# Output gate before reciprocal: VectorE multiplies numerator and gate into x's tile, GpSimd scales by the reciprocal in place

## Chip, cores and metric

One core of a Trainium2 chip runs the whole kernel. The metric is the device time of one execution in microseconds, as the median of three runs. TensorE's granted clock is full (1.0) over the whole profiled execution.

## What is computed

An attention-like recurrence (mLSTM) over 4 batches, 8 heads, 768 positions and head dimension 40, then a soft mixture of experts, then a feed-forward block. The change lies in the first part. Cut to what matters:

```python
for t in range(S):
    C = f_stab * C + i_stab * outer(v_t, k_t)
    n = f_stab * n + i_stab * k_t
    h_tilde = C @ q_t
    denom = max(abs(n . q_t), 1.0)
    o = 1 / (1 + exp(-o_gate_t))
    y[t] = o * h_tilde / denom           # the product that the change regroups
x = y as (3072 tokens, 320)
logits = x @ phi ; d = softmax over tokens ; slot_input = d.T @ x ; ...
```

The kernel computes the recurrence chunk by chunk. For every token it gets a numerator row (320 values and, per head, one value for the denominator), the reciprocal of the denominator (8 values), and the sigmoid of the output gate (320 values); x is the product of the three.

## The kernel before

The 3072 tokens are 24 units of 128 tokens: 6 chunks of the sequence times 4 batches, unit u = 4 * chunk + batch. The loop over iterations i = 0 to 23 is software-pipelined by hand. Iteration i works on units i-2 to i+2 at once, and the order in which the steps are issued is a string of step names: `FIRST` for iterations 0 to 5, `ORDER[i % 4]` for 6 to 21, `LAST` for 22 and 23. Each engine executes its own instructions strictly in the order in which the strings issue them, and waits on semaphores where a tile is not ready or not free. I call an iteration by its kind, i mod 4, and four iterations a period.

The steps that matter, with engine and line in the kernel before:

- `numa`, `numb` (VectorE, L327 and L329): the numerators of unit i-1, from TensorE's sums `pr` and `po` in PSUM, into `num`, of which there is one tile. `po` and `pr` are one PSUM tile each, so TensorE's first product of the next unit into `po` waits for `numb`.
- `den0`, `den2` (VectorE, L337 and L341): denominator and reciprocal `rd` of unit i-1; two `rd` tiles in turn.
- `sg` (VectorE, L345): sigmoid of the output gate times `rd`, in place in the tile `kvo` (or `kvl`) of the unit.
- `x` (GpSimd, L360): `num` times that product, into the unit's x tile. There are five x tiles, unit u has tile u mod 5 (names `x` and `xx` in the rows).
- `xT` (TensorE, L365): transposes x of unit i-2.
- `sl` (TensorE, L439), in iterations of kind 2: the slot sums of four units that are complete, which read their x tiles. In iteration i they read the x tiles of units i-6 to i-3, and the x written in the same iteration is that of unit i-1. Unit i-1 and unit i-6 have the same x tile.
- `acc` (VectorE, L447, the first time L445): adds the slot sums, in iterations of kind 2.
- `scA`, `scB` (TensorE, L280): scores of unit i+1; `wA`, `wB` (VectorE, L284): scores times decay, into `lb`. The score tiles in PSUM are single, so the next `scA` waits for both.
- `o0` to `o3` (TensorE, L298 and L301): outputs of unit i from `lb` and the state. `u0` to `u3` (L308): state updates.
- `cd` (GpSimd, L316): decayed state; `C` (VectorE, L356): the new state. `kw` (GpSimd, L269): weights on the keys of unit i+1, read by `u0` to `u3` of the next iteration.
- `D0` to `D4`: decoding of a weight tile, over two iterations. `D0` (L477, L478), `D3` (L486) and `D2` (L484) are VectorE's, `D1b` and `D1` ScalarE's, `D4` (L488) GpSimd's.
- L200 and L202 (VectorE, in `gate`): two small gate steps at the start of iterations 8, 12 and 16.

All loads are issued by SyncE in program order, ahead of their use. After iteration 23 come the expert part (a short stretch bound by TensorE and by what each step hands to the next) and the feed-forward part over 24 units.

The x step of the kernel before reads:

```python
x = x_t[u % NX]
(V if u == NU - 1 else EE("x")).tensor_tensor(out=x[:, 0:DM]..., in0=U[u]["num"][:, :, 0:D], in1=U[u]["sg"], op=ALU.mult)
```

Of the kernel before, what the change touches and what calls it, by code (L numbers as in the profile page):

```python
# [14 lines left out]
ALU = mybir.AluOpType  # L15
# [3 lines left out]
NB, NH, S, D = 4, 8, 768, 40  # L19
T = TOK = 128  # L20
NC = S // T
NU = NB * NC
NR = NH // 2
DV = D + 1
DM = NH * D
# [5 lines left out]


ORDER = (
# [4 lines left out]
)  # L38
LAST = (
 "numa xT tm1 scA numb scB den0 xTc tm2 nt ntc sig0 R o0 den2 o1 exp sg sig1 kw o3 wA wB o2 sl qm x sig2",  # L40
# [2 lines left out]
FIRST = (  # L43
# [6 lines left out]
)  # L50
# [6 lines left out]
FIN = "o:-1 u:2 d:2 t:2 h:3 m:3 q:0 k0:0 T0:1 T1:1 k1:0 x0:1 g:1 x1:1 y1:0 y0:1 k2:0 k3:0 s:0 a4:0 a5:0 e:3 a6:0 a7:0 v:1 b4:0 b5:0 b6:0 b7:0"  # L57
DT = range(2, 24)
HALF = (slice(0, 64), slice(64, 128))
ENG = {"x": "G", "cd": "G", "kw": "G", "sg": "V", "D4": "G", "C": "V", "xTc": "A"}  # L60


@with_exitstack
def tile_kernel(
# [13 lines left out]
    nc = tc.nc  # L78
    EE = lambda n: {"V": nc.vector, "G": nc.gpsimd, "A": nc.scalar}[ENG[n]]
    V, A, G, PE, SP = nc.vector, nc.scalar, nc.gpsimd, nc.tensor, nc.sync  # L80
# [19 lines left out]
    acc = cpool.tile([128, DM + 1], F32, tag="acc", name="acc")  # L100
# [24 lines left out]
    def fixed(name, shape, n=1, dtype=F32):  # L125
        t = [p1.tile(shape, dtype, tag=f"{name}{i}", name=f"{name}{i}") for i in range(n)]
        return t if n > 1 else t[0]

    NX = 5
    x_t = fixed("x", [128, 384], 2)  # L130
# [42 lines left out]
    U = [dict() for _ in range(NU)]  # L173
# [157 lines left out]
    def st_den(u, k):  # L331
# [8 lines left out]
        else:  # L340
            V.reciprocal(out=rd, in_=rd)  # L341

    def st_sg(u):
        sg = U[u]["kvo"][:, 2 * DM + NH:].rearrange("p (h d) -> p h d", h=NH)
        EE("sg").tensor_tensor(out=sg, in0=sg, in1=U[u]["rd"].unsqueeze(2).to_broadcast([128, NH, D]), op=ALU.mult)  # L345
        U[u]["sg"] = sg

    def st_state(u):
# [7 lines left out]
            V.tensor_tensor(out=C_t[b][0:n], in0=U[u]["cd"][0:n], in1=dps[0:n], op=ALU.add)  # L356

    def st_x(u):
        x = x_t[u % NX]
        (V if u == NU - 1 else EE("x")).tensor_tensor(out=x[:, 0:DM].rearrange("p (h d) -> p h d", h=NH), in0=U[u]["num"][:, :, 0:D], in1=U[u]["sg"], op=ALU.mult)  # L360

    def pe_xT(u):
        ps = ps_o.tile([128, 512], F32, tag="misc", name=f"xTp{u}")
# [257 lines left out]
    def ops(i):  # L621
# [13 lines left out]
        if prv:  # L635
            T["numa"] = lambda: st_num(i - 1, (0,))
            T["numb"] = lambda: st_num(i - 1, (1,))
            T["C"] = lambda: st_state(i - 1)
            for k in range(3):
                T[f"den{k}"] = lambda k=k: st_den(i - 1, k)  # L640
            T["sg"] = lambda: st_sg(i - 1)
            T["x"] = lambda: st_x(i - 1)
# [100 lines left out]
    def bank(tag, name):  # L743
        return ps_o.tile([128, 512], F32, tag=tag, name=name)
# [8 lines left out]
    U[L]["sg"] = kvo_t[L % 4][:, 2 * DM + NH:].rearrange("p (h d) -> p h d", h=NH)  # L753
    st_den(L, 0)
    st_x(L)
    st_den(L, 2)
    xl = x_t[L % NX][:, 0:DM].rearrange("p (h d) -> p h d", h=NH)
# [6 lines left out]
    xT = U[L]["xT"] = xT_t[L % 4]  # L764
# [9 lines left out]
    st, lt = gst_t[g % 2], lg[:, 0:128]  # L774
# [17 lines left out]
    sl = [bank(t, f"sl_last{k}") for k, t in enumerate(("dps", "po"))]  # L792
# [275 lines left out]
    for t in FIN_START.split():  # L1068
        op, i = t.split(":")
# [3 lines left out]
    for i in range(NU + 1):  # L1073
        for t in FIN.split():
            op, d = t.split(":")
# [78 lines left out]
```

## Time and profile before

| | us |
|---|---|
| median of 3 runs | 287.72 (286.51 to 288.02) |
| the profiled execution | 284.2 |
| its span, first to last instruction | 282.4 |

| engine | busy us | share of the span |
|---|---|---|
| TensorE, matmuls | 267.7 | 95% |
| VectorE | 243.1 | 86% |
| ScalarE | 216.9 | 77% |
| GpSimd | 149.6 | 53% |

The shares are averages over stages. Iterations 6 to 21, which the change touches, lie at about 39 to 126 us of the span; 16 of the 24 units are gone through there, in four periods of about 21.5 us. The feed-forward part fills the span from about 166 us on and issues its own instructions, which the change leaves as they are. What the change does to the time is therefore read from the four periods: which engine is waited for there, and where.

### The profile page before, as it was taken

To read this page: it belongs to the slowest core of one execution; us is meant where nothing else is said; L and a number is where in the kernel's file an instruction comes from. 1 tells how busy PE (TensorE), PEld (TensorE's weight loads), DVE (VectorE), ACT (ScalarE), POOL (GpSimd) and SP (SyncE) were. 2 spreads that over 40 slices of the span, in tenths; PEclk is the share of its full clock that TensorE was granted. 3 is DMA by queue.
4 is the path that set the end of the run, shared out by engine and by line. 5 is a ranking of instruction groups with operands and counts; after the bars stand their busy time and mean duration, and the time that the engine had idled before them with its cause. 6 is when DMAs were issued, how large, how long until landed. Compare 5 with 4: busy or idle time off the path is not lost.

```text
span 282.4 us, 8484 instructions
## 1 busy us (share of the span) xinstructions
PE 267.7 (95%) x3293; PEld 216.9 (77%) x3293; DVE 243.1 (86%) x514; ACT 216.9 (77%) x513; POOL 149.6 (53%) x179
## 2 busy tenths in 40 slices
PE   8899989999999999999899998999999999999995
PEld 5676767777777776867533367998999999999994
DVE  7999787998998997996579699999999999899950
ACT  6798957998789786797436758996877878778763
POOL 5754433654555555348106400556868767676760
PEclk9999999999999999999999999999999999999999
DMA  5898997999999998999999100246445364443531
GB/s 156 276 290 296 311 318 277 317 300 269 296 313 285 300 282 263 295 260 381 364 362 360 51 0 2 60 89 129 106 94 111 84 99 100 91 105 94 99 86 46
DMA packets 48808, 56.63 MB, mean 201 GB/s; under 512 B 26816, under 2 KB 38720, under 8 KB 48768
## 3 DMA queue, kind: packets, MB, share of 16 engines
q1 hardware_dynamic: 48768, 56.09, 67.6%
q8 instruction: 26, 0.43, 0.6%
q14 instruction: 14, 0.11, 0.1%
HBM read 46.38 MB, written 3.93 MB: 178 GB/s over the span
## 4 chain that ended last, share of the span: by engine, by line
PE 78%; DVE 6%; ACT 5%; issue 4%; DMA 4%; POOL 3%; POOLq 0%; ACTq 0%; SPq 0%; DVEq 0%
PE o L1046 9%; PE o L1043 9%; PE o L1044 9%; PE sc L280 8%; PE po L298 7%; PE R L244 4%; PE pr L301 4%; PE uT L1008 4%; PE h L962 3%; PE ph L836 3%; PE xTp L365 3%; PE so_ps L893 3%; DMA w2s<-w 3%; PE R L247 2%; PE dps L308 2%
## 5 line engine op out<-in xcount | busy, mean ns | idle before, releaser
L1043 PE MATMUL o<-wh,uh 128*128 128x320 f32 x192 | 60.3, 320 | 0.3 <-POOL uh L1029 0.3
L1044 PE MATMUL o<-wl,uh 128*128 128x320 f32 x192 | 58.2, 309 | 0.0
L1046 PE MATMUL o<-wh,ul 128*128 128x320 f32 x192 | 47.9, 310 | 0.1
L1014 POOL COPY up<-u 128x1024 uint16<-128x1024 uint16 x22 | 23.3, 1058 | 33.4 <-issue 16.1
L1024 POOL COPY uf<-tp 128x1024 uint16<-128x1024 uint16 x22 | 32.1, 1458 | 10.2 <-DMA tp<-up 10.1
L1043 PEld LDWEIGHTS o<-wh,uh 128*128 128x128 f32 x192 | 36.1, 188 | 1.5 <-POOL uh L1029 0.6
L1044 PEld LDWEIGHTS o<-wl,uh 128*128 128x128 f32 x192 | 36.1, 188 | 0.9
L1046 PEld LDWEIGHTS o<-wh,ul 128*128 128x128 f32 x192 | 33.0, 188 | 0.6 <-DVE ul L1035 0.6
L284 DVE TENSOR_TENSOR lb<-sc,lb 128x512 f32<-128x512 f32 x48 | 31.1, 674 | 1.9 <-PE sc L280 1.9
L967 DVE TENSOR_REDUCE st<-h 128x1 f32<-128x1024 f32 x24 | 29.2, 1220 | 0.3 <-PE h L962 0.2
L298 PE MATMUL po<-kvo,lb 128*64 128x41 f32 x544 | 27.2, 227 | 2.0 <-issue 2.0
L253 ACT ACTIVATE lb<-R 64x512 f32<-64x512 f32 (+1 forms) x48 | 25.5, 580 | 2.7 <-PE R L247 2.6
L1050 ACT ACTIVATE ob<-o,st 128x320 f32<-128x320 f32 x24 | 12.7, 529 | 18.9 <-ACT ga L974 8.4
L298 PEld LDWEIGHTS po<-kvo,lb 128*64 128x64 f32 x544 | 22.4, 137 | 5.1 <-issue 3.4
L280 PE MATMUL sc<-qk 64*128 64x128 f32 x288 | 23.1, 289 | 0.0
L280 PEld LDWEIGHTS sc<-qk 64*128 64x128 f32 x288 | 18.6, 187 | 4.2 <-issue 2.7
L1035 DVE TENSOR_TENSOR ul<-uf,uh 128x512 fp32r<-128x512 f32 x22 | 20.7, 941 | 1.2 <-POOL uh L1029 1.2
L981 DVE SCALAR_TENSOR_TENSOR u<-h,ga 128x1024 f32<-128x1024 f32 (+1 forms) x17 | 19.6, 1157 | 2.0 <-ACT ga L974 1.8
L1035 DVE TENSOR_TENSOR ul<-uT,uh 128x512 fp32r<-128x512 f32 x26 | 17.8, 684 | 2.8 <-ACT uh L1031 2.7
L261 ACT ACTIVATE kvo<-kvo 128x320 f32<-128x320 f32 x36 | 17.0, 472 | 3.8 <-DMA kvo<-kvo 1.9
L301 PE MATMUL pr<-C,qk 128*64 128x82 f32 x224 | 19.5, 249 | 0.0
L244 PE MATMUL R<-gr,gl 128*128 128x512 f32 x48 | 17.3, 442 | 1.1 <-ACT lb L253 1.1
(285 smaller groups left out, 708.9 us busy)
## 6 DMA issues: line engine op xcount, KB each, us to landing
w1s<-w1p SPq DMA_DIRECT2D x19, 512.0 KB
w2s<-w SPq DMA_DIRECT2D x7, 1280.0 KB
kvo<-kvo SPq DMA_DIRECT2D x15, 484.0 KB
out<-ob SPq DMA_DIRECT2D x24, 160.0 KB
qk<-qkp SPq DMA_DIRECT2D x18, 160.0 KB
qk<-qkp SPq DMA_DIRECT2D x36, 80.0 KB
kvl<-kvo SPq DMA_DIRECT2D x5, 484.0 KB
raw<-w SPq DMA_DIRECT2D x4, 512.0 KB
```

Source lines behind the costliest of these rows:

```text
L244: PE.matmul(U[u]["R"][:, a], gl_t[c % 2][:, b, :], gr_t[c % 2][:, a * NR:(a + 1) * NR, :], start=True, stop=False)
L253: A.activation(out=lb[p, :, :, t], in_=U[u]["R"][p, :, :, t], func=AF.Exp)
L280: PE.matmul(U[u]["sc", a][:, r, :], t[p, 0, r, :], t[p, 1, r, :], start=True, stop=True)
L284: V.tensor_tensor(out=lb[:, a * NR:(a + 1) * NR, :], in0=U[u]["sc", a], in1=lb[:, a * NR:(a + 1) * NR, :], op=ALU.mult)
L298: PE.matmul(U[u]["po"][t, 2 * r + a, 0:DV], U[u]["lb"][:, a * NR + r, t], va(u, 2 * r + a), start=not last or r + a == 0, stop=not last)
L301: PE.matmul(U[u]["po" if last else "pr"][t, 2 * r:2 * r + 2, 0:DV], qk_t[u % 4][:, 1, r, t], C_t[b][:, r, :].rearrange("p (a d) -> p a d", ...
L967: V.tensor_reduce(out=F[i]["st"][:, 0:1], in_=F[i]["h"], axis=AX.XY, op=ALU.max, negate=True)
L1024: G.tensor_copy(out=uf.rearrange("p k t -> p (k t)").bitcast(U16).rearrange("p (n two) -> p n two", two=2), in_=F[i]["tp"].rearrange("p tw ...
L1035: V.tensor_tensor(out=F[i]["ul"][:, c, :], in0=F[i]["uT", n], in1=F[i]["uh"][:, c, :].bitcast(F32), op=ALU.subtract)
L1043: PE.matmul(o, uh, wh[:, k, :], start=k == 0, stop=False)
L1044: PE.matmul(o, uh, wl[:, k, :], start=False, stop=False)
L1046: PE.matmul(o, ul, wh[:, k, :], start=False, stop=k == FC - 1)
```

## The change

In units 5 to 20 the three factors of x are grouped in another way. Before, VectorE multiplied gate and reciprocal (`sg`), and GpSimd multiplied the numerators by that. Now `sg` stands for VectorE's product of numerators and gate, written into the unit's x tile, and `x` for GpSimd's multiplication of that tile by the reciprocal, in place. The number of instructions on each engine stays as it was. The first five and the last three units keep the old grouping.

The order strings move with it. `sg` goes directly behind `numb` in kinds 0, 1 and 3; in kind 2 it stays behind `sl`. `x` goes to directly behind the reciprocal (or, in kind 2, behind `sg`), and `cd` goes ahead of `x`; `kw` and `D4` stand behind `x` on GpSimd where they had stood ahead of it.

```diff
@@ ORDER @@
- "R D1b D1 sig0 numa D2 scA C xT scB numb den0 den1 o0 u0 xTc left exp den2 wB o3 o2 gn sg wA cd o1 gnc sig1 x D0 u1 u2 u3 kw sig2 right",
- "D1b xT C numa numb R scA D1 den0 den1 xTc D3 den2 sig0 right left D2 scB kw sg wA o0 wB x u1 cd o3 lt o2 sig1 u3 o1 u2 D4 exp lraw ltc u0 tm0 sig2",
- "numa D1b xT tm1 scA numb D1 C scB den0 xTc tm2 D2 nt ntc sig0 den1 R o0 den2 o1 gn gnc sl sg sig1 u3 kw o3 wA wB cd o2 x exp acc u1 u2 u0 D0 sig2 right",
- "D1b xT numa R C numb scA D3 D1 scB o0 den0 sig0 cd den1 u3 D2 den2 wA D4 o3 u0 sig1 sg exp wB xTc u1 u2 o1 o2 lraw x sig2 kw right",
+ "R D1b D1 sig0 numa D2 scA C xT scB numb sg den0 den1 o0 u0 xTc left exp den2 cd wB o3 o2 gn x wA o1 gnc sig1 D0 u1 u2 u3 kw sig2 right",
+ "D1b xT C numa numb sg R scA D1 den0 den1 xTc D3 den2 cd sig0 right left D2 scB x kw wA o0 wB u1 o3 lt o2 sig1 u3 o1 u2 D4 exp lraw ltc u0 tm0 sig2",
+ "numa D1b xT tm1 scA numb D1 C scB cd den0 xTc tm2 D2 nt ntc sig0 den1 R o0 den2 o1 gn gnc sl sg x sig1 u3 kw o3 wA wB o2 exp acc u1 u2 u0 D0 sig2 right",
+ "D1b xT numa R C numb sg scA D3 D1 scB o0 den0 sig0 cd den1 u3 D2 den2 x wA D4 o3 u0 sig1 exp wB xTc u1 u2 o1 o2 lraw sig2 kw right",
...
@@ ENG: one entry more @@
+ "gate": "V"
...
+    def xh(u):
+        return x_t[u % NX][:, 0:DM].rearrange("p (h d) -> p h d", h=NH)
+
+    def rd_wide(u):
+        return U[u]["rd"].unsqueeze(2).to_broadcast([128, NH, D])
+
+    def early(u):
+        return len(FIRST) - 1 <= u < NU - 3
+
     def st_sg(u):
         sg = U[u]["kvo"][:, 2 * DM + NH:].rearrange("p (h d) -> p h d", h=NH)
-        EE("sg").tensor_tensor(out=sg, in0=sg, in1=U[u]["rd"].unsqueeze(2).to_broadcast([128, NH, D]), op=ALU.mult)
+        if early(u):
+            EE("gate").tensor_tensor(out=xh(u), in0=U[u]["num"][:, :, 0:D], in1=sg, op=ALU.mult)
+            return
+        EE("sg").tensor_tensor(out=sg, in0=sg, in1=rd_wide(u), op=ALU.mult)
         U[u]["sg"] = sg
...
     def st_x(u):
-        x = x_t[u % NX]
-        (V if u == NU - 1 else EE("x")).tensor_tensor(out=x[:, 0:DM].rearrange("p (h d) -> p h d", h=NH), in0=U[u]["num"][:, :, 0:D], in1=U[u]["sg"], op=ALU.mult)
+        if early(u):
+            EE("x").tensor_tensor(out=xh(u), in0=xh(u), in1=rd_wide(u), op=ALU.mult)
+        else:
+            (V if u == NU - 1 else EE("x")).tensor_tensor(out=xh(u), in0=U[u]["num"][:, :, 0:D], in1=U[u]["sg"], op=ALU.mult)
```

How this moves instructions, at two places. First VectorE, from the reciprocal of iteration 10 (kind 2) into iteration 11 (kind 3). The columns are line, operation, output and inputs, size, and the engines whose semaphores it waits for. Before:

```order
L341 RECIPROCAL rd_113<-rd_113 128x8 [waits DVE_49]
L345 TENSOR_TENSOR kvo_117<-kvo_117,rd_113 128x320 [waits DMAHW7_49,DVE_49]
L284 TENSOR_TENSOR lb_0_124<-sc_0_1113,lb_0_124 128x512 [waits PE_49]
L284 TENSOR_TENSOR lb_0_124<-sc_1_1114,lb_0_124 128x512 [waits PE_49]
L447 SCALAR_TENSOR_TENSOR acc<-acc,gst_102,sl_1157 128x321 [waits PE_49,Activation_49]
L477 TENSOR_SCALAR dsc_118<-raw_96 128x512 [waits DMAHW3_49,Pool_49]
L478 TENSOR_SCALAR wo<-raw_96 128x512
L327 TENSOR_TENSOR num_114<-pr_1143,nat_110 128x8x41 [waits PE_49,Pool_49]
L356 TENSOR_TENSOR C_122<-cd_119,dps 104x328 [waits PE_49]
L329 TENSOR_TENSOR num_114<-num_114,po_1142 128x8x41 [waits DVE_49]
L486 SCALAR_TENSOR_TENSOR dsc_118<-raw_96,dsc_118 128x512 [waits Activation_49]
L337 TENSOR_REDUCE rd_112<-num_114 128x8 [waits DVE_49]
```

The same stretch in the changed kernel (L355 is the product of numerators and gate, L461 is `acc`, L368 `C`, L500 and L498 are `D3` and `D2`):

```order
L341 RECIPROCAL rd_113<-rd_113 128x8 [waits DVE_49]
L355 TENSOR_TENSOR xx_100<-num_114,kvo_117 128x320 [waits DMAHW7_49,PE_49]
L284 TENSOR_TENSOR lb_0_124<-sc_0_1113,lb_0_124 128x512
L284 TENSOR_TENSOR lb_0_124<-sc_1_1114,lb_0_124 128x512
L461 SCALAR_TENSOR_TENSOR acc<-acc,gst_102,sl_1158 128x321 [waits PE_49,Activation_49]
L491 TENSOR_SCALAR dsc_118<-raw_96 128x512 [waits DMAHW3_49,Pool_49]
L492 TENSOR_SCALAR wo<-raw_96 128x512
L327 TENSOR_TENSOR num_114<-pr_1144,nat_110 128x8x41 [waits DVE_49,PE_49]
L368 TENSOR_TENSOR C_122<-cd_119,dps 104x328 [waits PE_49,Pool_49]
L329 TENSOR_TENSOR num_114<-num_114,po_1143 128x8x41 [waits DVE_49]
L355 TENSOR_TENSOR x_94<-num_114,kvo_116 128x320 [waits DMAHW5_49,DVE_49]
L500 SCALAR_TENSOR_TENSOR dsc_118<-raw_96,dsc_118 128x512 [waits Activation_49]
```

Before, L345 at the first place touches only `kvo` and `rd`, and behind `numb` of iteration 11 comes `D3`. Now L355 writes `xx_100` there and waits for PE, ahead of the two `lb` instructions and `acc`; a second L355 stands between `numb` and `D3`, and no instruction stands between `lb`'s two halves any more.

Second GpSimd, at the same place: from `cd` of iteration 10 to `kw` of iteration 11. Before:

```order
L316 TENSOR_TENSOR cd_119<-C_122,nat_110 104x328 [waits DVE_49]
L360 TENSOR_TENSOR xx_100<-num_114,kvo_117 128x320 [waits DVE_49,PE_49]
L316 TENSOR_TENSOR cd_119<-C_123,nat_110 104x328 [waits DVE_49,Pool_49]
L488 TENSOR_TENSOR wo<-wo,dsc_118 128x512 [waits DVE_49]
L360 TENSOR_TENSOR x_94<-num_114,kvo_116 128x320 [waits DVE_49,PE_49,Activation_49]
L269 TENSOR_TENSOR kvl_130<-kvl_130,nat_111 128x320 [waits DMAHW0_49]
```

In the changed kernel (L372 is the multiplication by the reciprocal, L502 is `D4`):

```order
L316 TENSOR_TENSOR cd_119<-C_122,nat_110 104x328 [waits DVE_49]
L372 TENSOR_TENSOR xx_100<-xx_100,rd_113 128x320 [waits DVE_49]
L269 TENSOR_TENSOR kvo_115<-kvo_115,nat_110 128x320 [waits DMAHW2_49]
L316 TENSOR_TENSOR cd_119<-C_123,nat_110 104x328 [waits DVE_49]
L372 TENSOR_TENSOR x_94<-x_94,rd_112 128x320 [waits DVE_49,PE_49]
L502 TENSOR_TENSOR wo<-wo,dsc_118 128x512
L269 TENSOR_TENSOR kvl_130<-kvl_130,nat_111 128x320 [waits DMAHW0_49,Activation_49]
```

Before, `D4` came ahead of x of iteration 11 and waited for VectorE on its own; now x comes first and `D4` directly ahead of `kw`. The `kw` of iteration 10 (on `kvo_115`) stood ahead of these rows and now stands behind the x of that iteration.

## Rows read from the trace of the kernel before

**Rows 1.** Busy time by engine in one period of four iterations, columns named.
```profile
core 0: us, PE busy (x) PEld busy (x) DVE busy (x) ACT busy (x) POOL busy (x), PEclk, DMA share, GB/s
...
79.30:100.80 21.50, 20.87 (x396) 16.30 (x395) 20.58 (x45) 18.18 (x49) 11.98 (x15) 1.00 0.96 293
```

**Rows 2.** Waits of VectorE, 36 to 127 us: total us, times, longest.
```profile
DVE acc L447 <- PE sl L439: 3.3, 3, 1.5
DVE acc L445 <- PE sl L439: 2.1, 1, 2.1
DVE num L327 <- POOL xx L360: 0.4, 1, 0.4
```

**Rows 3.** VectorE's instructions, 59 to 76 us: start, duration, line, tiles, wait before.
```profile
59.24 0.68 DVE L486 SCALAR_TENSOR_TENSOR dsc<-w1s,dsc 128x512 int32<-128x512 int32 x1
...
60.51 0.48 DVE L345 TENSOR_TENSOR kvl<-kvl,rd 128x320 f32<-128x320 f32 x1
60.91 1.28 DVE L284 TENSOR_TENSOR lb<-sc,lb 128x512 f32<-128x512 f32 x2
...
63.93 0.20 DVE L341 RECIPROCAL rd<-rd 128x8 f32<-128x8 f32 x1
...
64.85 1.27 DVE L284 TENSOR_TENSOR lb<-sc,lb 128x512 f32<-128x512 f32 x2
67.27 0.55 DVE L447 SCALAR_TENSOR_TENSOR acc<-acc,gst,sl 128x321 f32<-128x321 f32 x1 [1.15 <-PE sl L439]
...
69.27 0.48 DVE L329 TENSOR_TENSOR num<-num,po 128x328 f32<-128x328 f32 x1
69.67 1.09 DVE L486 SCALAR_TENSOR_TENSOR dsc<-raw,dsc 128x512 int32<-128x512 int32 x1
70.69 0.16 DVE L337 TENSOR_REDUCE rd<-num 128x8 f32<-128x16 f32 x1
...
72.04 1.11 DVE L345 TENSOR_TENSOR kvo<-kvo,rd 128x320 f32<-128x320 f32 x1
73.08 0.68 DVE L284 TENSOR_TENSOR lb<-sc,lb 128x512 f32<-128x512 f32 x1
73.68 0.59 DVE L200 TENSOR_TENSOR ga<-ga 32x128 f32<-32x128 f32 x1
74.20 0.70 DVE L202 TENSOR_TENSOR dec<-cst,ga 32x16 f32<-32x16 f32 x1
...
75.64 0.48 DVE L329 TENSOR_TENSOR num<-num,po 128x328 f32<-128x328 f32 x1
```

**Rows 4.** TensorE's instructions at the same place, columns alike.
```profile
66.61 0.43 PE L439 MATMUL sl<-xx,dn 128*32 128x321 f32 x1
...
68.18 0.55 PE L365 MATMUL xTp<-cst,xx 128*128 128x128 f32 x3
...
76.22 0.43 PE L298 MATMUL po<-kvl,lb 128*64 128x41 f32 x8 [0.58 <-PE sc L280]
...
88.04 0.44 PE L439 MATMUL sl<-x,dn 128*32 128x321 f32 x2
```

**Rows 5.** GpSimd's instructions at the same place, columns alike.
```profile
67.11 0.81 POOL L360 TENSOR_TENSOR xx<-num,kvo 128x320 f32<-128x320 f32 x1 [1.59 <-PE sl L439]
69.49 0.73 POOL L316 TENSOR_TENSOR cd<-C,nat 104x328 f32<-104x328 f32 x1 [1.57 <-DVE C L356]
71.53 1.27 POOL L488 TENSOR_TENSOR wo<-wo,dsc 128x512 f32<-128x512 f32 x1 [1.31 <-DVE wo L484]
73.32 0.80 POOL L360 TENSOR_TENSOR x<-num,kvo 128x320 f32<-128x320 f32 x1 [0.52 <-DVE kvo L345]
74.08 0.79 POOL L269 TENSOR_TENSOR kvl<-kvl,nat 128x320 f32<-128x320 f32 x1
```

**Rows 6.** TensorE in iterations 20 and 21.
```profile
119.12 0.43 PE L298 MATMUL po<-kvl,lb 128*64 128x41 f32 x8
...
121.46 0.55 PE L365 MATMUL xTp<-cst,xx 128*128 128x128 f32 x3 [0.62 <-POOL xx L360]
```

More of the change, by code (lines that the diff above doesn't have):

```diff
@@ L59 @@
 HALF = (slice(0, 64), slice(64, 128))
-ENG = {"x": "G", "cd": "G", "kw": "G", "sg": "V", "D4": "G", "C": "V", "xTc": "A"}
+ENG = {"x": "G", "cd": "G", "kw": "G", "sg": "V", "gate": "V", "D4": "G", "C": "V", "xTc": "A"}
 @with_exitstack
```

## Prediction

> **What bounds the kernel now.** I read the stage table first. In iterations 6 to 21 TensorE is busy 20.87 of 21.50 us in a period, VectorE 20.58, and the DMA engines 0.96 of the time [rows 1]; none has room for much. So the question is not what an engine has to do, but who waits for whom. VectorE's waits come next: it waits nearly only at one place, once in each of the four periods, in front of `acc` for TensorE's slot sums `sl`: 2.1 us in the first period and 3.3 us in the other three together [rows 2]. Third I laid the instructions of VectorE, TensorE and GpSimd side by side from iteration 10 to 14 and looked for the loop that sets the period.
>
> It is this. `sl` of iteration 10 ends at 66.61 + 0.43 = 67.04 [rows 4]. `acc` starts 0.23 later at 67.27, and from there VectorE works without a gap until `numb` of iteration 12 ends at 75.64 + 0.48 = 76.12 [rows 3]. TensorE has then been idle for 0.58, because the one `po` tile is not free before `numb` has read it, and goes on 0.10 later at 76.22; without another gap it ends `sl` of iteration 14 at 88.04 + 0.44 = 88.48 [rows 4]. 0.23 + 8.85 + 0.10 + 12.26 = 21.44 us, which is the period. Whatever is put on VectorE between `sl` and that `numb` lengthens it one to one. Ahead of `sl`, on the other hand, VectorE has time to spare: the reciprocal of iteration 10 is done at 63.93 + 0.20 = 64.13, and `sg` and both `lb` products stand between it and `acc` and are done while `sl` is still coming [rows 3].
>
> **What the change does to that loop.** The change adds no instruction and removes none; it moves work from one side of `sl` to the other.
>
> *Kind 2.* The new VectorE product writes the x tile that `sl` of the same iteration is still reading (unit i-1 and unit i-6 share it). Before, that wait was GpSimd's, whose x started at 67.11 after 1.59 us of waiting [rows 5]; now it is VectorE's, and behind the waiting instruction are queued both `lb` products and `acc`. VectorE would be there at 64.13 and stands until about 67.11. Then come the product (0.40 from start to start, as `sg` from 60.51 to 60.91) and two `lb` products (0.60 each, 73.08 to 73.68) [rows 3], and `acc` starts at 67.11 + 0.40 + 1.20 = 68.71 instead of 67.27: **+1.44 us**. The same instructions used to be hidden by the wait; that cover is gone.
>
> *Kind 3.* From `acc` to `numb` of iteration 11 nothing changes (2.00 us, to 69.27) [rows 3], so `numb` starts at 70.71. The product behind it has two inputs in SBUF, and `cd` starts on GpSimd 0.22 behind `numb` and takes 0.73 [rows 5]. Two such instructions do not run side by side: the `sg` of 72.04 met `D4` (71.53 + 1.27 = 72.80), took 1.11 instead of 0.48 and ended 0.35 after it [rows 3, 5]. So `cd` lasts to 71.66, the product to 72.01, and it costs 71.94 - 71.11 = +0.83. In exchange `D3`, which stood beside `cd` with 1.09, is back to 0.68: -0.41. And `sg` between the `lb` halves goes, with 73.08 - 72.04 = -1.04 [rows 3]. Sum -0.62, balance +0.82: the second `lb` half is done and L200 is reached at 74.50 instead of 73.68.
>
> *L200 and L202* open iterations 8, 12 and 16. They meet GpSimd too: L202, 16 columns wide, takes 0.70 beside `kw`, and ends 0.03 behind it (74.90 and 74.87) [rows 3, 5]. In the new order x starts on GpSimd about 0.17 after the reciprocal (about 73.4, as the first `lb` half begins), so at about 73.55; `D4` 0.76 behind it at 74.3, until 75.58. L200 arrives 0.2 too late for the gap and ends 0.15 behind `D4` (as behind x before), at 75.73; `kw` then runs from 75.54 to 76.33 and L202 ends at 76.36 instead of 74.90: +0.64 more, balance **+1.46**. `numb` ends at 77.58, TensorE's `o0` starts at 77.68, and the period is 21.44 + 1.46.
>
> The Trainium skill has a rule for these meetings ("SBUF — State Buffer", section "Who interferes with whom"): a VectorE instruction with two SBUF inputs and a GpSimd instruction that reads SBUF exclude each other for the whole instruction, and the one that issues first goes first. The rows on `sg` and `D4` agree. By that rule L200 waits for all of `D4`, as in my sum; if the two could overlap, the sum would be +2.7 instead of +4.6.
>
> *Kinds 0 and 1.* There the product behind `numb` replaces `sg` behind the reciprocal, and in kind 0 `cd` meets it. All this lies on the part of the loop where TensorE is without a gap and VectorE arrives at the next `sl` some 2.5 us early, so I cost it at nothing.
>
> *What else moves.* x of kind 2 comes later (product, then GpSimd, about 68.5); the transposition that reads it starts at 68.18 [rows 4] and waits some 0.4, but TensorE has to wait longer than that for `numb` of iteration 11 a little later, so nothing. `kw` in kind 2 comes after x instead of before it, at about 69.2, ahead of the state updates that read it. In the other kinds x is done earlier. The wait of `num` for GpSimd disappears, 0.4 us in all [rows 2]. The `kvo` tile is free earlier, so SyncE's loads are issued earlier or at the same time.
>
> **The sum.** Three whole loops (`sl` of 6 to 10, 10 to 14, 14 to 18; the others show the pattern of the one I laid out, the `acc` wait of each included): 3 x 1.46 = 4.4. The fourth ends in iteration 20, which has no L200 and L202: TensorE's `o0` at 119.12 comes 0.82 later; but its 0.62 wait for x at 121.46 [rows 6] goes, since x no longer comes behind `sg`: +0.2. Together **+4.6 us**. After that everything (the last units, the loads for the expert part, which wait for tiles that TensorE frees, and the feed-forward part) follows TensorE and shifts as a whole. On the profiled execution's 284.2 us this makes 288.8; that execution lies 3.5 below the median of the runs shown, and with the same shift the median goes from 287.72 to **292.3**.
>
> **Rivals.**
>
> *A, smaller.* L200 slips in front of `D4`, or `D4` is late itself. Then 3 x 0.82 + 0.2 = +2.7: 290.4. For it: the order is decided by 0.2 us. Against: `D4` then holds L202 instead.
>
> *B, larger.* `kw` goes ahead of L200 as well (+0.3), VectorE wakes as late after `sl` as `acc` does (67.27 instead of 67.11, +0.16), and the wait in iteration 21 is not regained: 3 x 1.92 + 0.82 = +6.6: 294.3.
>
> *C, no change.* The loads set the pace, and compute only waits elsewhere. For it: DMA busy share 0.96 [rows 1]. Against: TensorE goes on 0.10 behind VectorE's `numb`, not behind a load. Then 287.7.
>
> *D, faster.* The wait for `sl` never shows, because VectorE comes to the product after `sl`. Then only the gains stay: 0.62 in each of three loops and the 0.62 of iteration 21, 287.72 - 2.5 = 285.2. It decides at VectorE being 67.04 - 64.13 = 2.9 us later at that place than now; nothing moves it by so much, since VectorE's delay delays `sl` as well.
>
> **How the numbers follow.** Forecast 60%, A 15%, B 12%, C 8%, D 5%. The predicted time is the forecast's, 292.3. The range holds A and B and leaves out C and D, with 0.8 below A and 0.3 above B, since the runs themselves lie 1.5 apart: 289.6 to 294.6. This kernel's measurement can tell about 0.5% (1.4 us) from no change. Faster by more than that: D, 5%. Within it: C and the lowest of A, 10%. Slower: 85%.
>
> **What would show it.** Right: in the profile after, VectorE's line for the new product is the one that waits for `sl`, nearly 3 us each of four times, and `acc` no longer waits; from `sl` of 10 to `sl` of 14 are 22.9 us instead of 21.44; `o0` of iteration 12 starts 0.1 behind `numb` and after an idle time of over 1 us; L200 and L202 together take over 1.7 us; the product in kind 3 takes about 0.9, `D3` 0.68. Wrong: no wait at the product (D), or a period of 21.4 with the wait there (C), or TensorE stopped somewhere else, for instance at the state updates for `kw`, which I have cost at nothing.

## The result, and the profile after

The changed kernel takes 288.53 us (median of 20 runs, 286.67 to 293.27), the kernel before 285.74 beside it (median of 20 runs, 283.10 to 290.96). The ratio is 1.0106 [1.0076, 1.0137]: 3.0 us slower, 2.2 to 3.9 (the ratio's ends less 1, times 285.74). The sign and the place were as predicted; 288.53 lies below the range of 289.6 to 294.6. Medians here are over all runs, and ratios over those that lie within 1.5% of their kernel's fastest, so the two differ a little.

In the profile that is shown here, TensorE waited 1.7 us for late loads of `qk` in iteration 6 and then had a granted clock of 0.50 for 3.4 us. Up to these loads both kernels issue the same instructions, so I compare from the end of `sl` in iteration 6 on. I call the stretch from the end of one `sl` to the end of the next a loop; there are three, and the prediction's is the middle one. Busy time by engine in the three loops of the kernel before (the first column is the stretch, the first number behind it its length):

```profile
core 0: us, PE busy (x) PEld busy (x) DVE busy (x) ACT busy (x) POOL busy (x), PEclk, DMA share, GB/s
45.13:67.04 21.91, 21.17 (x398) 16.54 (x398) 20.61 (x44) 19.78 (x54) 11.94 (x14) 1.00 0.92 293
67.04:88.48 21.44, 20.86 (x399) 16.36 (x399) 20.51 (x44) 17.77 (x47) 11.91 (x14) 1.00 0.95 298
88.48:110.59 22.11, 21.08 (x398) 16.38 (x399) 20.32 (x44) 17.46 (x46) 11.97 (x14) 1.00 0.95 288
```

The same view of the changed kernel:

```profile
49.98:72.59 22.61, 20.65 (x399) 16.11 (x398) 19.55 (x44) 19.41 (x53) 11.38 (x14) 1.00 0.92 276
72.59:95.25 22.66, 20.66 (x399) 16.11 (x399) 19.43 (x44) 18.11 (x49) 11.39 (x14) 1.00 0.89 301
95.25:117.90 22.65, 20.65 (x397) 16.10 (x398) 19.65 (x44) 17.45 (x46) 11.38 (x14) 1.00 0.83 283
```

All three engines of the chain are busy for less time than before (VectorE 19.43 instead of 20.51, TensorE 20.66 instead of 20.86, GpSimd 11.39 instead of 11.91), and the loop is 1.22 longer. The three loops of the changed kernel are alike within 0.05; those of before are not, and that matters below. The differences are +0.70, +1.22 and +0.54. From the last `sl` to the transposition of iteration 21 it is 11.09 instead of 10.87, +0.22. The sum is 2.68, about the whole difference in time. The kernel before has only one kept profile, so its lengths are those of one execution; those of the changed kernel repeat in e1.

VectorE's waits from 36 to 127 us, which answer to [rows 2]:

```profile
DVE xx L355 <- PE sl L453: 7.6, 3, 2.5
DVE x L355 <- PE sl L453: 6.7, 1, 6.7
```

The wait in front of `acc` is gone, and the new product has it, 2.5 us in each of the three later places (the 6.7 holds the stop in iteration 6). VectorE in the middle loop, which answers to [rows 3] (start, duration, line, tiles, wait before):

```profile
69.87 0.20 DVE L341 RECIPROCAL rd<-rd 128x8 f32<-128x8 f32 x1
72.61 0.49 DVE L355 TENSOR_TENSOR xx<-num,kvo 128x320 f32<-128x320 f32 x1 [2.54 <-PE sl L453]
73.02 1.28 DVE L284 TENSOR_TENSOR lb<-sc,lb 128x512 f32<-128x512 f32 x2
74.22 0.54 DVE L461 SCALAR_TENSOR_TENSOR acc<-acc,gst,sl 128x321 f32<-128x321 f32 x1
...
76.16 0.49 DVE L329 TENSOR_TENSOR num<-num,po 128x328 f32<-128x328 f32 x1
76.68 0.72 DVE L355 TENSOR_TENSOR x<-num,kvo 128x320 f32<-128x320 f32 x1
77.32 0.68 DVE L500 SCALAR_TENSOR_TENSOR dsc<-raw,dsc 128x512 int32<-128x512 int32 x1
...
79.86 1.17 DVE L200 TENSOR_TENSOR ga<-ga 32x128 f32<-32x128 f32 x1
80.97 0.70 DVE L202 TENSOR_TENSOR dec<-cst,ga 32x16 f32<-32x16 f32 x1
...
82.41 0.48 DVE L329 TENSOR_TENSOR num<-num,po 128x328 f32<-128x328 f32 x1
```

TensorE and GpSimd at the same place, which answer to [rows 4] and [rows 5]:

```profile
72.14 0.44 PE L453 MATMUL sl<-x,dn 128*32 128x321 f32 x2
...
74.90 0.52 PE L379 MATMUL xTp<-cst,xx 128*128 128x128 f32 x3 [1.10 <-DVE acc L461]
...
82.98 0.43 PE L298 MATMUL po<-kvl,lb 128*64 128x41 f32 x8 [0.89 <-PE sc L280]
```

```profile
76.32 0.73 POOL L316 TENSOR_TENSOR cd<-C,nat 104x328 f32<-104x328 f32 x1 [1.72 <-DVE C L368]
78.93 0.72 POOL L372 TENSOR_TENSOR x<-x,rd 128x320 f32<-128x320 f32 x1 [1.89 <-DVE rd L341]
79.61 1.28 POOL L502 TENSOR_TENSOR wo<-wo,dsc 128x512 f32<-128x512 f32 x1
```

The reader is to see the loop that the prediction laid out, with other lengths. `sl` ends at 72.59, the product, both `lb` and `acc` follow, VectorE has no gap until `numb` ends at 82.89, and `o0` starts 0.09 later. From there to the next end of `sl` it is 12.27, as before (12.26). Only VectorE's stretch grew, from 9.08 to 10.30.

New to me is `xTp` at 74.90: TensorE stood 1.10 for `acc`. The transposition writes the PSUM tile that `sl` was in, and `acc` now reads that late. It costs nothing here, since TensorE stands 0.89 more for `numb` later on; without the first wait it would stand some 2 us at `o0` (an estimate, 1.10 + 0.89).

### The profile page after: what moved, and what is told of

It is laid out like the page before. It is cut to its first block, busy times and chain, and to the rows that moved or that the text cites. A ratio compares the mean times of both kernels' runs of the same rounds, so it can differ in the third digit from the quotient of the medians.

```text
span 290.0 us, 8472 instructions
## 1 busy us (share of the span) xinstructions
PE 268.4 (93%) x3293; PEld 216.9 (75%) x3293; DVE 237.3 (82%) x514; ACT 216.4 (75%) x513; POOL 148.2 (51%) x179
## 4 chain that ended last, share of the span: by engine, by line
PE 65%; DMA 10%; issue 8%; DVE 8%; POOL 5%; ACT 3%; SPq 1%; POOLq 0%; DVEq 0%; ACTq 0%
PE o L1060 8%; PE o L1057 8%; PE o L1058 8%; PE sc L280 6%; DMA qk<-qkp 6%; PE po L298 5%; PE uT L1022 3%; PE R L244 3%; PE ph L850 3%; PE so_ps L907 3%; PE h L976 3%; PE pr L301 3%; PE xTp L379 3%; DMA kvl<-kvo 2%; PE R L247 2%
## 5 line engine op out<-in xcount | busy, mean ns | idle before, releaser
L1038 POOL COPY uf<-tp 128x1024 uint16<-128x1024 uint16 x22 | 33.1, 1503 | 9.9 <-DMA tp<-up 9.8
L284 DVE TENSOR_TENSOR lb<-sc,lb 128x512 f32<-128x512 f32 x48 | 30.5, 677 | 1.2 <-PE sc L280 0.9
L298 PE MATMUL po<-kvo,lb 128*64 128x41 f32 x544 | 26.6, 227 | 0.8 <-PE sc L280 0.8
L298 PEld LDWEIGHTS po<-kvo,lb 128*64 128x64 f32 x544 | 21.8, 138 | 3.7 <-issue 1.0
L1049 DVE TENSOR_TENSOR ul<-uf,uh 128x512 fp32r<-128x512 f32 x22 | 19.7, 894 | 1.3 <-POOL uh L1043 1.2
```

Of the source, the lines that this page charges most:

```text
L284: V.tensor_tensor(out=lb[:, a * NR:(a + 1) * NR, :], in0=U[u]["sc", a], in1=lb[:, a * NR:(a + 1) * NR, :], op=ALU.mult)
L298: PE.matmul(U[u]["po"][t, 2 * r + a, 0:DV], U[u]["lb"][:, a * NR + r, t], va(u, 2 * r + a), start=not last or r + a == 0, stop=not last)
L1038: G.tensor_copy(out=uf.rearrange("p k t -> p (k t)").bitcast(U16).rearrange("p (n two) -> p n two", two=2), in_=F[i]["tp"].rearrange("p tw ...
L1049: V.tensor_tensor(out=F[i]["ul"][:, c, :], in0=F[i]["uT", n], in1=F[i]["uh"][:, c, :].bitcast(F32), op=ALU.subtract)
```

## Experiments

Theory 1 is the prediction's: the new wait for `sl` in kind 2 and what is queued behind it sets the loop. Theory 2: the loss comes from the late loads of `qk` in iteration 6. Theory 3: it comes from L200 and L202 meeting `D4`. Theory L came with e9: the loads had already made two loops of the kernel before longer. Each kernel has one profile, so a single loop may be that execution's. Lengths of the loops are taken from the end of `sl` to the end of `sl`, as above.

| kernel | loop 1 | loop 2 | loop 3 | ratio to before [95%] |
|---|---|---|---|---|
| before | 21.91 | 21.44 | 22.11 | |
| changed | 22.61 | 22.66 | 22.65 | 1.0106 [1.0076, 1.0137] |
| e1 changed, again | 22.59 | 22.66 | 22.65 | 1.0137 [1.0081, 1.0193] |
| e2 kind 2 as before | 21.38 | 21.63 | 21.85 | 0.9991 [0.9947, 1.0035] |
| e3 `lb` ahead of the product | 22.28 | 25.23 | 22.28 | 1.0058 [1.0019, 1.0097] |
| e4 six x tiles | 21.51 | 21.27 | 22.36 | 1.0034 [0.9989, 1.0079] |
| e5 kind 2 alone changed | 22.65 | 22.71 | 22.71 | 1.0173 [1.0085, 1.0262] |
| e6 changed, gate steps in the wait | 21.62 | 21.69 | 25.22 | 1.0067 [1.0018, 1.0116] |
| e7 before, gate steps in the wait | 21.15 | 20.80 | 25.45 | 1.0108 [1.0023, 1.0193] |
| e8 as e2, gate steps in the wait | 20.74 | 22.33 | 27.23 | 0.9966 [0.9882, 1.0049] |
| e9 before, five loads later | 21.43 | 21.44 | 21.88 | 1.0072 [1.0026, 1.0117] |
| e10 changed, five loads later | 22.59 | 22.65 | 22.65 | 1.0173 [1.0100, 1.0246] |
| e11 as e7, five loads later | 22.76 | 20.79 | 20.80 | 1.0117 [1.0068, 1.0166] |

### e1: the changed kernel once more

No edit.

> The changed kernel once more, unaltered, beside the next three on the same chip. Theory 1 (VectorE's product in kind 2 waits for the slot sums, with both lb products and acc queued behind it): about 3 us slower than before (ratio 1.008 to 1.014), and in the profile three loops of 22.65 us from slot sum to slot sum. Theory 2 (the loads of qk that held TensorE up before iteration 6 in the first profile of the changed kernel carry the loss): the loss varies from profile to profile with that stall, and without the stall it is under 1 us.

287.98 us beside 285.54, the loops within 0.02 of the first profile's. The loss and its place repeat.

### e2 and e5: kind 2 undone, and kind 2 alone

e2 gives kind 2 its old order and old grouping and leaves kinds 0, 1 and 3 changed; e5 takes the new kind 2 alone into the kernel before.

```diff
 e2, in the changed kernel
- ... o1 gn gnc sl sg x sig1 u3 kw o3 wA wB o2 exp acc ...
+ ... o1 gn gnc sl sg sig1 u3 kw o3 wA wB cd o2 x exp acc ...
-        return len(FIRST) - 1 <= u < NU - 3
+        return len(FIRST) - 1 <= u < NU - 3 and u % 4 != 1
 e5, in the kernel before: the new kind 2 line, and
+        return len(FIRST) - 1 <= u < NU - 3 and u % 4 == 1
```

> The changed kernel with the old grouping and the old order in iterations of kind 2 alone; kinds 0, 1 and 3 stay changed. Theory 1: the loss goes, since no VectorE instruction in front of the lb products waits for the slot sums: between 1 us faster and 0.5 us slower than before (0.62 us less on VectorE in kind 3 in each of three loops, against up to 0.6 more at L200 and L202). Theory 3 (the meeting of D4 with L200 and L202 carries most of the loss, 0.58 of 1.22 us in a loop): about 1.7 us slower remain. Theory 2 (loads): as the changed kernel, about 3 us slower.

> The kernel before with the new grouping and the new order in iterations of kind 2 alone (units 5, 9, 13, 17), kinds 0, 1 and 3 as before. Theory 1: the whole loss comes from here. acc comes 1.40 us later after the slot sums than before, kind 3 keeps the sg that meets D4; three loops of about 22.8 to 23.2 us, and the time is 2.5 to 4.5 us over that of before (ratio 1.009 to 1.016). Theory 3 (L200 and L202 meeting D4 in the new order of kind 3 carry most): at most 1.5 us slower, since kind 3 is as before.

e2: 285.18 us beside 285.54, no difference. `acc` waits for `sl` again and runs 0.24 behind its end (69.92 in this profile):

```profile
70.16 0.55 DVE L461 SCALAR_TENSOR_TENSOR acc<-acc,gst,sl 128x321 f32<-128x321 f32 x1 [0.62 <-PE sl L453]
```

e5: 290.09 beside 287.38. Busy time by engine in its middle loop (columns as above):

```profile
69.31:92.02 22.71, 21.03 (x398) 16.39 (x398) 20.04 (x44) 18.10 (x49) 11.78 (x14) 1.00 0.87 299
```

Kind 2 alone lengthens this loop by 1.27, the whole change by 1.22. So the loss is in kind 2, and what kinds 0, 1 and 3 gain and lose on VectorE nearly cancels in this loop: of the 0.77 gained between `acc` and L200, 0.58 goes back at L200 and L202 (below). They do save time at the end: in e5 the transposition of iteration 21 comes 12.16 behind the last `sl`, still with the wait of 0.62 for x, and in the changed kernel 11.09. Theories 2 and 3 fail: by theory 3 e5 should have lost at most 1.5 us, and by both e2 should have kept a loss.

### e3: the queued products put ahead of the product

```diff
- ... sl sg x sig1 u3 kw o3 wA wB o2 exp acc ...
+ ... sl sig1 u3 o3 wA wB sg x kw o2 exp acc ...
```

> The changed kernel, but in kind 2 both lb products stand ahead of the new product, so that the wait for the slot sums holds up only the product itself and acc. Theory 1: of the 1.40 us by which acc comes later in a loop, about 0.4 stay (the product itself), so about 1 us of the loss of 3 remains, 0 to 1.5 us slower than before. Theory 2 or 3: no difference to the changed kernel of more than 0.5 us.

286.40 us beside 285.54: by the ratios (1.0058 and 1.0137) less than half of the loss of e1 is left. Its loops 1 and 3 are 22.28 (in loop 2 the granted clock was 0.50 for 6.83 us). VectorE at `sl` of iteration 10, which ends at 70.79, and GpSimd beside it:

```profile
68.22 1.29 DVE L284 TENSOR_TENSOR lb<-sc,lb 128x512 f32<-128x512 f32 x2
70.81 0.49 DVE L355 TENSOR_TENSOR xx<-num,kvo 128x320 f32<-128x320 f32 x1 [1.30 <-PE sl L453]
71.22 0.55 DVE L461 SCALAR_TENSOR_TENSOR acc<-acc,gst,sl 128x321 f32<-128x321 f32 x1
71.68 0.71 DVE L491 TENSOR_SCALAR dsc<-raw 128x512 int32<-128x512 int32 x1
72.31 0.96 DVE L492 TENSOR_SCALAR wo<-raw 128x512 int32<-128x512 int32 x1
```

```profile
71.38 0.72 POOL L372 TENSOR_TENSOR xx<-xx,rd 128x320 f32<-128x320 f32 x1 [2.62 <-DVE xx L355]
72.06 0.92 POOL L269 TENSOR_TENSOR kvo<-kvo,nat 128x320 f32<-128x320 f32 x1
```

`acc` comes 0.43 behind `sl` instead of 1.63: 1.20, the two `lb`, is off the path. But the loop is only 0.37 shorter than the changed kernel's 22.65. The rows show where 0.84 went: `D0` (L491 and L492, 0.34 and 0.33 from start to start in the changed kernel) now stands beside x and `kw` on GpSimd and takes 0.63 and 0.88. In the changed kernel x and `kw` ran beside the `lb` products, which read their scores from PSUM and took no longer there (1.28 for both). The Trainium skill says under "SBUF — State Buffer", section "Who interferes with whom", that a tensor_scalar can enter a mode that takes the ports that VectorE shares with GpSimd; these rows agree (0.71 and 0.96 instead of 0.42).

### e4: the wait taken away by a sixth x tile

```diff
-    NX = 5
+    NX = 6
-    d_t = fixed("d", [128, 128])
-    dn_t = fixed("dn", [128, 128])
+    d_t = dn_t = gp_t.bitcast(F32)
```

The last three lines make room for the tile: `d`, `dn` and an early gate tile now share one.

> The changed kernel with six x tiles instead of five, the order untouched; room for the sixth is made by letting two small tiles of the slot softmax share one with an early gate tile. The x written in kind 2 is then not one that the slot sums still read, and the wait is taken away without moving an instruction. Theory 1: the product in kind 2 starts right behind the reciprocal, acc waits for the slot sums again, and the time is that of before or up to 1.5 us faster. Theory 2 or 3: still 1.5 to 3 us slower than before.

286.41 us beside 285.54, ratio 1.0034 [0.9989, 1.0079]. The product no longer waits and runs 2.6 ahead of the end of `sl` (66.36); `acc` comes 0.23 behind it, as in the kernel before:

```profile
63.75 0.93 DVE L354 TENSOR_TENSOR xx<-num,kvo 128x320 f32<-128x320 f32 x1
64.60 1.28 DVE L283 TENSOR_TENSOR lb<-sc,lb 128x512 f32<-128x512 f32 x2
66.59 0.55 DVE L460 SCALAR_TENSOR_TENSOR acc<-acc,gst,sl 128x321 f32<-128x321 f32 x1 [0.71 <-ACT lb L252]
```

The wait is the cause: with the same instructions in the same order and one tile more, the loops are back near those of the kernel before (65.14 in sum, 65.46 before, 67.92 in the changed kernel), and no loss clear of the noise is left. From `sl` of iteration 6 to the transposition of iteration 21 this profile takes 75.08 instead of 76.33, but only 0.30 of the 1.25 is left at the first product of the feed-forward part (`h`, 120.90 instead of 121.20 behind the same `sl`). In the expert part before it TensorE waits 0.3 for a weight (`w2s`), which the kernel before does not. The rest of that, and loop 3 (22.36 with TensorE busy 21.89), I have not followed.

### e6, e7 and e8: the gate steps put into the wait

If VectorE's work between `sl` and `numb` sets the loop, L200 and L202 can be moved out of it. They are taken from the start of iterations 8, 12 and 16 and put in front of the wait for `sl` in iterations 6, 10 and 14: in the changed kernel (e6), in the kernel before (e7) and in e2 (e8).

```diff
-            if ng > 1:
+            if ng == 2:
...
+        if i % 4 == 2 and 6 <= i < 18:
+            T["g78"] = lambda: [gate(((i + 2) // 4 + 1) * TOK, ((i + 2) // 4 + 2) * TOK, k) for k in (7, 8)]
 e6:  ... den2 g78 o1 gn gnc sl ...
 e7, e8:  ... wA wB g78 cd o2 ...
```

> The changed kernel with L200 and L202 two iterations earlier, behind the reciprocal in kind 2, where VectorE waits for the slot sums anyway. Theory 1: they leave the loop (1.73 us from L200 to numb in the changed kernel), so the loop falls from 22.65 until the next bound holds, which I put at TensorE's 20.9 to 21.4 us of work and small waits: three loops of 21.0 to 21.6, and the time is between 2 us under and 0.5 us over that of before. If VectorE between slot sums and numb does not set the period, nothing changes: 3 us slower.

> The kernel before with the same move: L200 and L202 behind the lb products of kind 2, in front of acc, where VectorE waits for the slot sums. Theory 1: 1.15 us leave the loop of 21.44 (20.3 on VectorE), TensorE's work of about 20.9 then holds: three loops of 20.9 to 21.4, 0.5 to 2.5 us faster than before (ratio 0.991 to 0.998), less whatever the loads of w2s give back. If the loads set the period: no change.

> Both at once: the changed kernel with kind 2 as before, and L200 and L202 in the wait of kind 2. Theory 1: the shortest loop on VectorE of all (another 0.6 us less in kind 3), but TensorE's own work holds by then: three loops of 20.8 to 21.2; 1 to 3 us faster than before, less what the loads of w2s give back (in the run with six x tiles TensorE waited for one of them in the expert part).

287.25, 288.09 and 288.41 us beside 287.38. The whole times are a miss: e7 and e8 were to be faster than the kernel before, and e6 at most 0.5 us slower. By their ratios e6 and e7 are 0.7% and 1.1% slower, and e8 can't be told from it. In loops 1 and 2 it is as theory 1 has it: against the changed kernel e6 is 0.99 and 0.97 shorter, and against the kernel before e7 is 0.76 and 0.64 shorter. In e6, 1.73 of work went out of VectorE's stretch, and the loop is only 0.97 shorter: now TensorE's new wait for `acc`, which had lain under the other, is the one that ends last. It is TensorE's only wait in that loop:

```profile
69.03 0.52 PE L379 MATMUL xTp<-cst,xx 128*128 128x128 f32 x3 [1.10 <-DVE acc L461]
```

But loop 3 took 25 us and more in all three profiles, and more was lost there than had been gained before. e8's profile is disturbed in loop 2 too. Busy time in e7's loops 2 and 3, then its stretch around 107 us, then TensorE's rows and GpSimd's `kw` there:

```profile
67.99:88.79 20.80, 20.80 (x399) 16.33 (x399) 19.73 (x44) 17.99 (x49) 11.87 (x14) 1.00 0.95 314
88.79:114.24 25.45, 22.75 (x398) 17.59 (x398) 20.15 (x42) 17.95 (x46) 12.28 (x14) 0.93 0.89 274
```

```profile
106.00:108.30 2.30, 0.05 (x3) 0.01 (x1) 1.14 (x4) 0.20 (x1) 1.72 (x2) 1.00 0.79 296
108.30:109.94 1.64, 1.64 (x21) 1.42 (x21) 1.20 (x4) 0.86 (x3) 0.65 (x1) 1.00 1.02 335
109.94:113.35 3.41, 3.41 (x36) 2.54 (x33) 1.64 (x3) 2.44 (x8) 1.03 (x2) 0.50 0.70 217
```

```profile
105.73 0.32 PE L308 MATMUL dps<-kvo 128*40 128x41 f32 x6
108.30 0.27 PE L308 MATMUL dps<-kvo 128*40 128x41 f32 x2 [2.25 <-issue]
```

```profile
102.76 1.13 POOL L269 TENSOR_TENSOR kvo<-kvo,nat 128x320 f32<-128x320 f32 x1 [1.90 <-DMA kvo<-kvo]
109.29 0.74 POOL L269 TENSOR_TENSOR kvo<-kvo,nat 128x320 f32<-128x320 f32 x1 [1.58 <-DMA kvo<-kvo]
```

In loop 2 TensorE is never idle and the DMA engines are at 0.95 with 314 GB/s. In loop 3 TensorE stands 2.25 within the state updates. It goes on at a granted clock of 1.00 for 1.64 us, and then the clock is 0.50, the lower of its two levels (1.2 GHz), for 3.41 us. `kw` waits twice for a late load of `kvo`, but that is not what stops TensorE: the first of the two runs well before the stop and the second behind it, and the stop lies between the sixth and the seventh of eight matmuls, in the middle of a step whose matmuls read one tile. "issue" says that the profile shows nothing that TensorE waited for. The DMA engines are busy, so loads are the suspect all the same; e9 to e11 test it.

### e9, e10 and e11: five loads later

The first feed-forward weight is loaded in 512 KB pieces, one per iteration, and the pieces to be decoded come in the odd iterations beside them. Five pieces are moved from iterations 7 to 16 to iterations 18 to 21. This makes the later part of the kernel wait for loads, so the loops are compared and not the whole time.

```diff
-W1_UNITS = (1, 2, 3, 4, 4, 5, 5, 7, 8, 9, 10, 11, 12, 13, 14, 15, 16, 18, 22)
+W1_UNITS = (1, 2, 3, 4, 4, 5, 5, 8, 10, 12, 14, 16, 18, 19, 19, 20, 20, 21, 22)
```

> The kernel before, with one 512 KB load in each iteration from 7 to 16 instead of two in the odd ones: the loads of the first feed-forward weight that stood in iterations 7, 9, 11, 13 and 15 are postponed to iterations 18 to 21. All five come in the later part of the kernel, where they may cost up to some us, so the verdict on the whole time says little; the loops (end of sl to end of sl) are what is compared. Theory L, the first and third loop of the kernel before were longer than the middle one because loads of kvo came late (kw on GpSimd waited for one 0.9 us): without these loads all three loops come to 21.4 or a little below (sum of three 64.0 to 64.4 instead of 65.46). Rival M, they were longer for something else: 21.9, 21.4, 22.1 again, within 0.2 each.

> The changed kernel with the same loads postponed. If VectorE's order around sl alone sets its loop (theory 1), the loops stay at 22.6 each; with theory L the difference to the kernel before with the same loads is then 1.2 us in every loop, 3.6 in three, where the two kernels as they are differ by 0.70, 1.22 and 0.54. If loads held the changed kernel too (rival C of the prediction), its loops fall below 22.4.

> The kernel before with the two gate steps in the wait for sl (as e7) and the same loads postponed. Theory L: the third loop, which was 25.45 with TensorE stopped 2.3 us at dps, comes down to that of the first two, 20.8 to 21.2, and no wait of GpSimd's kw for a load of kvo above 1 us is left. If the stall had another cause than the loads, the third loop stays above 23.

The loops of e9, then of e10, then loops 2 and 3 of e11:

```profile
45.87:67.30 21.43, 20.85 (x397) 16.34 (x398) 20.58 (x44) 19.42 (x53) 12.05 (x14) 1.00 0.81 268
67.30:88.74 21.44, 20.87 (x399) 16.36 (x398) 20.50 (x44) 18.00 (x49) 12.05 (x14) 1.00 0.72 255
88.74:110.62 21.88, 20.74 (x398) 16.21 (x398) 20.60 (x44) 17.35 (x46) 12.04 (x14) 1.00 0.77 262
```

```profile
46.51:69.10 22.59, 20.65 (x397) 16.10 (x398) 19.54 (x44) 19.41 (x53) 11.39 (x14) 1.00 0.78 265
69.10:91.75 22.65, 20.66 (x399) 16.11 (x399) 19.43 (x44) 18.11 (x49) 11.38 (x14) 1.00 0.70 242
91.75:114.40 22.65, 20.65 (x397) 16.09 (x398) 19.66 (x44) 17.45 (x46) 11.38 (x14) 1.00 0.74 252
```

```profile
71.77:92.56 20.79, 20.79 (x398) 16.32 (x399) 19.73 (x44) 17.88 (x49) 12.01 (x14) 1.00 0.74 259
92.56:113.36 20.80, 20.80 (x398) 16.33 (x398) 19.46 (x42) 17.24 (x46) 12.01 (x14) 1.00 0.82 268
```

The changed kernel's loops do not move (22.59, 22.65, 22.65) while the DMA engines' share falls from 0.92, 0.89, 0.83 to 0.78, 0.70, 0.74: loads do not hold it, the order on VectorE does. In the kernel before, loop 1 falls from 21.91 to 21.43, as theory L expected and rival M did not. Loop 3 falls only from 22.11 to 21.88, since TensorE stands 1.14 in it, again with nothing named:

```profile
94.06 0.38 PE L298 MATMUL po<-kvo,lb 128*64 128x41 f32 x7 [1.14 <-issue]
```

The differences between the two kernels are now 1.16, 1.21 and 0.77. And e11's loop 3 is 20.80: with fewer loads the stop of e7 is gone. (Its first loop of 22.76 begins at a lower clock, after late loads of `qk`.)

Late `kw`, as theory L had it, are not the way in which the loads made these loops longer. In the kernel before, loop 1 is level with loop 2 to 0.02 until a stop of TensorE that ends at 65.52, and loop 3 until one that ends at 106.15 (an earlier stop in each is made up at the wait for `numb`). Behind them loops 1 and 3 are 0.48 and 0.67 late, which is all of their excess. The profile names nothing that TensorE waited for there. What these stops have in common is a queue that carries instructions:

```profile
q8 instruction: 26, 0.43, 0.6%
```

Its packets are 16 KB each and come some 7 us apart; the packed trace has their times. In all the loops there are ten unnamed stops of 0.18 us or more, without e3's waits at `o0`, which end 0.10 behind `numb`: four in the kernel before (to 50.91, 65.52, 92.84 and 106.15), three in e7 (to 52.44, 93.42 and 108.30) and one each in e4, e6 and e9 (to 50.80, 107.67 and 94.06). Every one ends 1.36 to 1.74 us behind the end of such a packet. At the stop in the state updates of loop 3 the packet starts 15.07 behind `sl` in the kernel before and 16.87 in e7, 1.80 later, and the stop ends 1.84 later (17.67 and 19.51 behind `sl`). In e9 and e11 the packet starts at 12.60 and 12.87, and TensorE does not stop there. So TensorE most likely waited for its own instructions, which came later with the five loads in place. No run moves these packets alone, and why one is late in e9 (2.59 behind `sl`, 1.79 before) stays open. The changed kernel shows no such stop in any of its three profiles.

The whole times are 288.19, 291.99 and 289.00 us beside 286.14: the postponed loads cost more later than the loops gain. No kernel here is faster than the kernel before by more than its interval.

## Why the prediction was right and wrong

**Right: the loop.** It is `sl`, product, `lb`, `acc`, then VectorE without a gap to `numb` of iteration 12, `o0`, `sl`. Its links measured 0.09 (forecast 0.1) behind `numb` and 12.27 behind that; the wait of 2.5 us sits at the new product; e2, e4 and e5 tie the loss to it. The idle time in front of `o0` was to be over 1 us and is 0.89, since TensorE already stood 1.10 for `acc`.

**Right but for small sizes: the price of the middle loop**, 1.22 instead of 1.46.

- Kind 2: `acc` at 74.22 is 1.63 behind `sl` instead of 0.23: +1.40 (forecast +1.44).
- From `acc` to `numb` of iteration 11: 1.94 instead of 2.00, -0.06 (forecast 0).
- Kind 3: from `numb` to `D3` 1.16 instead of 0.40, +0.76 (forecast +0.83); the product took 0.72 and ended at 77.40, 0.35 behind `cd`, as `sg` ended behind `D4` before [rows 3, 5]. From `D3` to L200 2.54 instead of 4.01, -1.47 (forecast -1.45). L200 was reached +0.63 later (forecast +0.82).
- L200 at 79.86 met `D4`, which had started at 79.61, took 1.17 and ended 0.14 behind it (forecast 0.15); with L202 it is 1.73 from start to start until the next `num` instead of 1.15, +0.58 (forecast +0.64). Rival A's way, L200 ahead of `D4`, did not happen.

**Right by luck: the end.** +0.22 from the last `sl` to the transposition of iteration 21 (forecast +0.2), but by another way. `o0` of iteration 20 was to come 0.82 later for `numb`. It comes 0.91 later (9.44 instead of 8.53 behind the last `sl`), and TensorE stood for `acc` in front of `xTp` (1.11 at 120.22); `numb` had ended at 126.47, 0.87 ahead of `o0`. The wait of 0.62 for x goes, as forecast. From there the later part has its old length: from the first `h` to the end of the span it is 116.14 us and was 116.07.

**Wrong: three times the middle loop.** "3 x 1.46 = 4.4", with the remark that the others show the pattern of the one laid out. Their pattern is the same, but in the profile that the prediction was read from their length was not: 21.91 and 22.11 instead of 21.44, which the other `sl` rows would have shown. The new wait doesn't add to that excess, it covers it: the changed kernel's loops are all 22.6. So the gains in length were 0.70, 1.22 and 0.54, 2.46 in sum instead of 4.38. Of the 1.92 that are missing, 0.72 is the price of the loop (3 x 0.24) and 1.20 is this cover (0.52 in loop 1, 0.68 in loop 3). The excess of before is two stops of TensorE, and in e9, with five loads moved, both are gone; loop 3 of e9 is still 0.44 longer than its loop 2 because of another stop. With one profile of the kernel before, the cover is that of one execution: the whole time, 2.2 to 3.9 us slower, fits it, but does not rule out three full prices (3 x 1.22 + 0.22 = 3.9).

**Wrong: the level.** The sum was put on the median of three runs, 287.72; over 20 runs the kernel before has 285.74. That is 2.0 of the 3.8 us between 292.3 and 288.53. The profiled execution's own 284.2, which the prediction named and passed over, would have given 288.8. The range had 0.8 us for all this, although the three runs alone lay 1.5 apart.

**Rival C, loads set the pace,** was rejected because TensorE goes on behind `numb` and not behind a load. For a loss that was right (e10). But e7 and e11 show that the loads are the next limit close by: in the loop that followed two of 21.15 and 20.80 us TensorE stopped for 2.25, and with five loads moved it did not. The prediction had no word on that, since it only looked for where the kernel gets longer.

**Costed at nothing:** `kw` behind x did no harm (no wait of TensorE's state updates in the changed kernel's loops). `xTp` was said to wait 0.4 for x; it waits 1.10, for `acc`, through a PSUM tile that the prediction hadn't followed. It was to be hidden by a wait for `numb` of iteration 11; that one does not appear (`o0` at 77.25 has no idle time in front of it). What hides it is the wait for `numb` of iteration 12, by luck of size: e6 shows `xTp` as the bound once that wait is shorter.

## What to carry to other kernels

An instruction that is put in front of a wait on an engine that works in order takes everything queued behind it into the wait: count what stood hidden there before, not the instruction itself, and see whether another buffer removes the wait (e4). Lay out every repetition of a loop before multiplying, since a new wait is partly paid by stalls that were there already. And ask of a shorter loop which resource comes next: in e7 a stop that went with the loads took back more than two loops had gained.

## What the runs showed of the hardware

- `D0`, a tensor_scalar over 512 columns, takes 0.42 alone and 0.71 and 0.96 beside GpSimd's x and `kw` (e3). I had counted only VectorE's instructions with two SBUF inputs as sensitive to GpSimd.
- GpSimd's product of 320 columns with the broadcast reciprocal takes 0.72, the old one with the strided numerators 0.81 [rows 5].
- TensorE can stop in the middle of a step with nothing named. Ten such stops of 0.18 to 2.25 us end 1.36 to 1.74 us behind a 16 KB packet of the instruction queue `q8`. In e7, at a DMA share of 0.95 in the loop before, one took 2.25; in e11, at 0.74, there is none.
- After TensorE's stop of 2.25 us in e7 its granted clock stayed 1.00 for 1.64 us and was then 0.50 (1.2 GHz) for 3.41, and the loop became 4.65 longer than the one before it, twice the stop. In e3 TensorE waits 1.14 to 1.15 at `o0` in each loop; behind the second wait the clock was 0.50 for 6.83 us, behind the first and the third it stayed 1.00. After the wait of 1.10 and 0.89 in each loop of the changed kernel it stays at 1.00 too.
